# Linformer attention and an MLP mixer on one core: batch 0's loads, its last head pair and its E and F in another order, and a planner's table in place of its shaken priorities

## The chip, the cores and the metric

The kernel runs on one core of a Trainium2 chip. The metric is the device time of one execution in microseconds (us); three runs of the kernel before gave 421.42, 422.15 and 422.19, with a median of 422.15. The engines are TensorE (PE; its weight loads are listed apart as PEld), VectorE (DVE), ScalarE (ACT), GpSimd (POOL) and SyncE (SP). A core has 16 DMA engines, which the queues of the engines share.

## The reference

Eight batches, eight heads, a sequence of 1024 and 64 elements a head. Attention is of the Linformer kind: k and v are first projected along the sequence to 64 rows by E and F. An MLP mixer follows, on x, which has 512 columns (eight heads side by side).

```python
k_proj = np.einsum('ks,bhsd->bhkd', E, k)
v_proj = np.einsum('ks,bhsd->bhkd', F, v)
scores = scale * np.matmul(q, k_proj.transpose(0, 1, 3, 2))
...
x = softmax(scores) @ v_proj                       # B, S, H * D
h = np.maximum(xt @ w_tok1, 0.0) @ w_tok2          # xt: x with S and columns exchanged, 1024 -> 256 -> 1024
u = x + h.transpose(0, 2, 1)
h2 = np.maximum(u @ w_ch1, 0.0) @ w_ch2            # 512 -> 1536 -> 512
return (u + h2).astype(np.float32)
```

All inputs and the output are float32 in the chip's memory; the kernel computes in bfloat16 with float32 sums.

## The kernel before

**Stages of a batch.** `kv_proj` (L479) multiplies k by E and v by F, both turned, in eight steps of 128 sequence rows; the k side and the v side use different halves of the array. ScalarE copies the result out, k to `kp` or `kb`, v to `vb`. `k_transpose` and `q_transpose_pe` (TensorE, batch 0 and 1) or DMA transposes on SP (L524, L570; from batch 2 on) bring q and k into the layout that `scores` (L605) needs; `attend` (L628) multiplies the softmax's numerators `a` by v, and VectorE divides (`rdn` L640, `x_sb` L645 and L681). `token1` and `token2` are the token MLP, in forms that differ by batch: in pairs of heads for batch 0 (`token1_pair`, `token2_pair`, L1067), plain for batch 1, in a seven-product scheme later (L744, L856). VectorE adds x to make `u` (L1079 in batch 0).

**The channel MLP** holds most of the work. u is transposed into `uT` (on TensorE in batch 0; by `turn_u`, L767, one DMA transpose on SP for each half of a batch after that). A half batch is a block j = 2b or 2b + 1. Each block does seven products of quarter matrices in place of eight, twice: `s_sums` (L789) makes the sums S of quarters on VectorE, `up_set` (L1152) the products to the hidden layer in two sets of columns, and `down_block` (L1261) the products back. Sums of weights (`wT`, `wc_sb`, L452) are made once. VectorE adds results and u into three tiles `o` (L1301, L1311), which rotate over half blocks, and `store` (L1295) writes an o tile out. Blocks with j under `EARLY_O` (4) put one part into `wait_t` first.

**The order of the work** is made when the program is built. A `Planner` (L50 to L203) holds jobs with an engine, a planned duration, a priority and the PSUM banks they take; it lists them in planned order. Priorities above `SHAKEN_FROM` are shifted by a hash of the job's number, within plus and minus 0.8. The list is then sorted by start; loads and stores (`early`) are sorted by the time at which their inputs or buffers are free, not by their planned start:

```python
j.at = est[j.n] if j.early else t
...
return sorted(order, key=lambda j: j.at)
```

Each engine's instructions stand in that order, and so do the DMA issues of each queue. Loads (`load_heads`, L363, issued at L354) and most stores go through GpSimd's queue, one behind another; the last blocks store through SP and ScalarE. Later batches' loads are 512 KB each (four heads of k, v or q). A group of three loads is tied (`tie`, L358; the wait is put in at L1503) behind a `turn_u`, and the second `turn_u` of a batch behind these loads, so that loads and DMA transposes take turns.

**The start.** E and F come in float32 through SP's and ScalarE's queues into two o tiles; they are turned with sixteen 64x64 transposes (L441) against `ident32`, which GpSimd makes after the first load's issue. Batch 0's loads stand in this order: k, v, q of head pairs 0, 1 and 2 (256 KB each), `wt1` (512 KB, the first token weight), k, v, q of pair 3, `wt2`, then the channel weights, then batch 1's six loads. Eight products on zeros (`blank`, L413) run while nothing has arrived; while bank 5 is free, the emitting loop (L1489) puts in one more for each 0.216 us of a planned hole on TensorE.

Of the kernel before, what the change touches and what calls it, by code (L numbers as in the profile page):

```python
# [14 lines left out]
SHAKEN_FROM = -30.0  # L15
SHAKE = 1.6
SEED = 710
# [7 lines left out]
EARLY_O = 4  # L25
# [3 lines left out]
class Job:  # L29


    def __init__(self, n, eng, occ, lat, fn, prio):
        self.n, self.eng, self.occ, self.lat, self.fn, self.prio = n, eng, occ, lat, fn, prio
        self.deps, self.next, self.takes, self.banks = set(), [], [], []
        self.start = self.end = None
        self.early = False
# [11 lines left out]
class Planner:  # L48


    LAG = {"PE": 0.25, "DVE": 0.15, "ACT": 0.15, "POOL": 0.2, "DMA": 1.0}
# [34 lines left out]
    def plan(self):  # L86
# [16 lines left out]
        for j in self.jobs:  # L103
            if j.prio > SHAKEN_FROM:
                j.prio += SHAKE * ((j.n * j.n * 7919 + j.n * SEED * 31 + SEED * SEED * 17) % 10007 / 10007 - 0.5)
# [19 lines left out]
        order = []  # L125
        turn = {n: [b for j in self.jobs for b in j.takes if b.stream == n] for n in self.caps}
# [28 lines left out]
        while any(can.values()):  # L155
# [23 lines left out]
            j.start, j.end, j.full = t, t + j.lat, t + j.lat + 0.03  # L179
# [27 lines left out]
def kernel(  # L207
# [66 lines left out]
    EF = [o_t[i].rearrange("p a b -> p (a b)")[:KP] for i in range(2)]  # L274
    nc.sync.dma_start(out=EF[0], in_=E)
    nc.scalar.dma_start(out=EF[1], in_=F)
# [18 lines left out]
    kp = wS[:KP, 0].rearrange("p a b -> p (a b)").rearrange("p (h r d) -> p h r d", h=H // 2, r=2)  # L295
    kb = tile_of([P, H, 2, D], BF16, "kb")
    ET_sb = tile_of([P, NSI, KP], BF16, "ET_sb")
    FT_sb = tile_of([P, NSI, KP], BF16, "FT_sb")
# [15 lines left out]
    ident32 = ub_t[0][:KP, 0, :KP]  # L314

    zero = tile_of([P, P], BF16, "zero")
    nc.vector.memset(zero, 0.0)
    nc.vector.memset(vb, 0.0)
# [12 lines left out]
    def pe(n, cols, fn, **kw):  # L331
        t = n * MM[cols]
        return pl.add("PE", t, t, fn, **kw)
# [12 lines left out]
    def ld(mb, fn, **kw):  # L346
        t = mb / 0.40
        j = pl.add("DMA", t, t + 2.0, fn, **kw)
        j.early = True
        return j  # L350
# [12 lines left out]
    def load_heads(b, name, h, hn, due):  # L363
        dst, src = {"k": (k_sb, k), "v": (v_sb, v), "q": (q_sb, q)}[name]
        hs = slice(h, h + hn)
        return ld(
            0.262 * hn,
            dma(dst[:, hs], src[b, hs].rearrange("h (p si) d -> p h si d", p=P)),
            writes=[(name, i) for i in range(h, h + hn)], prio=due,
        )  # L370
    first = iter(range(-1000, 0))
    for hp in range(HP):
        if hp == HP - 1:
            w1t = moe_w_tok1.rearrange("(p si) t -> p si t", p=P)
            ld(1.05, dma(wt1_sb, w1t), writes=["wt1"], prio=next(first))
        for name in "kvq":
            load_heads(0, name, 2 * hp, 2, next(first))
    w2t = moe_w_tok2.rearrange("(tc p) s -> p tc s", p=P)
    ld(1.05, dma(wt2_sb, w2t), writes=["wt2"], prio=next(first))
# [44 lines left out]
    for i in range(8):  # L424
        warm(i)
# [5 lines left out]
    pl.add("POOL", 1.0, 2.4, identities, writes=["ident"], prio=-150)  # L431

    for n, (src, dst) in enumerate(((EF[1], FT_sb), (EF[0], ET_sb))):
        b = Bank("S", full=False)

        def view(b=b):
            return bank(b).rearrange("p (si k) -> p si k", si=NSI)

        def turn(src=src, view=view):
            for si in range(NSI):  # L440
                nc.tensor.transpose(view()[:, si, :], src[:, si:S:NSI], ident32)  # L441

        def take(n=n, dst=dst, view=view):
            (nc.vector.tensor_copy if n else nc.scalar.copy)(out=dst, in_=view())

        pl.add("PE", 1.6, 1.6, turn, reads=["ident"], takes=[b], prio=-150)
        (dve if n else act)(512, take, writes=["FT", "ET"][n : n + 1], uses=[b], prio=-150)
# [31 lines left out]
    def kv_proj(b, h0, hn, due, block=False):  # L479
        hs = slice(h0, h0 + hn)  # L480
        hk = slice(h0 % (H // 2), h0 % (H // 2) + hn)
        heads = range(h0, h0 + hn)
        bk = Bank(stream[0], full=False)

        def view():
            return bank(bk).rearrange("p (h d) -> p h d", d=D)

        def mm(lo, hi):
            t = view()
            for si in range(lo, hi):  # L490
                a, z = si == 0, si == NSI - 1
                nc.tensor.matmul(  # L492
                    t[0:KP, 0:hn], ET_sb[:, si, :], k_sb[:, hs, si, :], start=a, stop=z
                )
                nc.tensor.matmul(
                    t[KP : 2 * KP, 0:hn], FT_sb[:, si, :], v_sb[:, hs, si, :], start=a, stop=z
                )

        cols = hn * D
        reads = ["ET", "FT"] + [(n, h) for n in "kv" for h in heads]  # L500
        pl.add(
            "PE", 8 * max(cols, 128) / 2400 + 0.22, 8 * max(cols, 128) / 2400 + 0.22,
            lambda: mm(0, NSI), reads=reads, takes=[bk], prio=due,
            after=[("vb", i, h) for i in range(2) for h in heads],
        )
        src = [lambda: view()[0:KP, 0:hn], lambda: view()[KP : 2 * KP, 0:hn]]
        if block:
            k_to = [kb[i * KP : (i + 1) * KP, hs, i, :] for i in range(2)]
        else:
            k_to = [kp[:, hk, i, :] for i in range(2)]  # L510
        v_to = [vb[i * KP : (i + 1) * KP, hs, i, 0:D] for i in range(2)]

        def copy(to, n):
            return lambda: nc.scalar.copy(out=to, in_=src[n]())

        for i in range(2):
            act(cols, copy(k_to[i], 0), writes=[("kb" if block else "kp", i, h if block else h % (H // 2)) for h in heads], uses=[bk])
        for i in (1, 0):
            act(cols, copy(v_to[i], 1), writes=[("vb", i, h) for h in heads], uses=[bk])
# [11 lines left out]
    def k_transpose(h0, hn, due):  # L531
# [7 lines left out]
        def mm():  # L539
            for h in range(hn):  # L540
                nc.tensor.matmul(
                    view()[:, h, :], kp[:, h0 % (H // 2) + h].rearrange("k r d -> k (r d)"),
# [4 lines left out]
            hn, 64, mm, reads=[("kp", i, h % (H // 2)) for i in range(2) for h in heads], takes=[bk],  # L547
# [142 lines left out]
    def token1(t, due):  # L690
# [9 lines left out]
        for part in range(2):  # L700
            pe(
                4, 512, lambda part=part: mm(part), reads=["wt1"] + [("x", h, part) for h in range(H)],
# [61 lines left out]
    def turn_u(b, i):  # L764
        turned_u[b, i] = sp(
# [9 lines left out]
        if b > 1:  # L775
            turned_u[b, i].lat += 3.0
# [23 lines left out]

    def tok1_quarter(t, half):
        return wt1_sb[:, half * NJ : (half + 1) * NJ, t * P : (t + 1) * P]

    def tok1_sums():
        a11, a12, a21, a22 = [tok1_quarter(t, half) for t in range(2) for half in range(2)]

        def one(n, out, in0, in1, add=False, deps=(), after=()):
# [3 lines left out]
                reads=["wt1"] + [("wS", m) for m in deps], writes=[("wS", n)], after=after,  # L811
            )

        kp_all = [("kp", i, h) for i in range(2) for h in range(H // 2)]
# [3 lines left out]
        one(6, wS[:, 1], wS[:, 0], a11, deps=(5,))  # L818
        one(3, a21, a12, wS[:, 1], deps=(6, 7, 5), after=["wt1"])
# [7 lines left out]
    def token1_seven(b, due):  # L827
# [35 lines left out]
        def product(n):  # L863
# [4 lines left out]
            w = [("wS", n)] if n in (5, 6, 7, 3) else ["wt1"]  # L868
# [162 lines left out]
    def token1_pair(hp, due):  # L1031
        cols = slice(hp * P, (hp + 1) * P)
        bk = Bank(stream[0], full=False)

        def view():
            return bank(bk)[:, 0 : TC * P].rearrange("p (t c) -> p t c", t=TC)

        def mm(t):
            for si in range(NSI):
                nc.tensor.matmul(  # L1040
                    view()[:, t, :], wt1_sb[:, si, t * P : (t + 1) * P], x_sb[:, si, cols],
                    start=(si == 0), stop=(si == NSI - 1),
                )

        for t in range(TC):
            pe(
                NSI, 128, lambda t=t: mm(t),
                reads=["wt1"] + [("x", 2 * hp + h, n) for h in range(2) for n in range(2)],
                takes=[bk] if t == 0 else [], uses=[bk] if t else [], prio=due,
            )  # L1050
        act(
            256,
            lambda: nc.scalar.activation(out=hT_sb[:, :, cols], in_=view(), func=ACT.Relu),
            writes=[("hT", t, hp) for t in range(TC)], uses=[bk],
        )

    def token2_pair(hp, i, due):
        cols = slice(hp * P, (hp + 1) * P)
        bk = Bank(stream[0], full=False)

        def view():
            return bank(bk).rearrange("p (s c) -> p s c", s=NJ)

        def mm():
            for ss in range(NJ):
                for t in range(TC):
                    nc.tensor.matmul(  # L1067
                        view()[:, ss, :], wt2_sb[:, t, i * NJ + ss :: NSI], hT_sb[:, t, cols],
                        start=(t == 0), stop=(t == TC - 1),
                    )  # L1070

        rows = slice(i * NJ, (i + 1) * NJ)
        pe(
            NJ * TC, 128, mm, reads=["wt2"] + [("hT", t, hp) for t in range(TC)], takes=[bk],
            prio=due,
        )
        dve(
            512,
            lambda: nc.vector.tensor_add(  # L1079
                out=u_t[0][:, rows, cols], in0=view(), in1=x_sb[:, rows, cols]  # L1080
            ),
            reads=[("x", 2 * hp, i), ("x", 2 * hp + 1, i)], writes=[("up", hp, i)], uses=[bk],
        )

    def u_transpose_pe(hp, i, due):
# [11 lines left out]
        pe(NJ, 128, mm, reads=[("up", hp, i)], takes=[bk], prio=due)  # L1097
# [437 lines left out]
```

## Time and profile before

| what | value |
|---|---|
| runs | 421.42, 422.15, 422.19 us |
| span of the profiled execution | 420.3 us |
| its own time | one of the runs above, 1.1 to 1.9 us over the span |
| TensorE busy | 410.3 us (98%), 3824 products |
| VectorE busy | 347.5 us (83%) |
| ScalarE busy | 231.3 us (55%) |
| GpSimd busy | 66.2 us (16%) |
| moved by the DMA engines | 62.48 MB, mean 149 GB/s |
| sixteen 64x64 transposes of E and F | 2.00 us, from 5.75 us |
| first S sum of block 0 ends | 35.95 us |
| kv_proj of batch 1, heads 4 to 7, starts | 55.46 us |
| kv_proj of batch 3, v side, starts | 110.04 us |

The slices of the page cut the span into 40 equal parts and give the busy share of each in tenths. The chain is followed back from the last instruction: at each step it goes to what released that step. A DMA on the chain means that an engine stood until that transfer had landed. In a timeline a row gives start, length, engine, line, tiles and, in brackets, the idle time before it and what ended it.

### The profile page before, as it was taken

To read this page: it belongs to the slowest core of one execution; us is meant where nothing else is said; L and a number is where in the kernel's file an instruction comes from. 1 tells how busy PE (TensorE), PEld (TensorE's weight loads), DVE (VectorE), ACT (ScalarE), POOL (GpSimd) and SP (SyncE) were. 2 spreads that over 40 slices of the span, in tenths; PEclk is the share of its full clock that TensorE was granted. 3 is DMA by queue.
4 is the path that set the end of the run, shared out by engine and by line. 5 is a ranking of instruction groups with operands and counts; after the bars stand their busy time and mean duration, and the time that the engine had idled before them with its cause. 6 is when DMAs were issued, how large, how long until landed. Compare 5 with 4: busy or idle time off the path is not lost.

```text
span 420.3 us, 9411 instructions
## 1 busy us (share of the span) xinstructions
PE 410.3 (98%) x3824; PEld 347.6 (83%) x3838; DVE 347.5 (83%) x747; ACT 231.3 (55%) x444; POOL 66.2 (16%) x104
## 2 busy tenths in 40 slices
PE   7899999999999999999999999999999999999996
PEld 4587877688788888888988898888798899988885
DVE  2359969679779798998979799797979999978685
ACT  2958885356646555555547455475655554454430
POOL 8443220022003030032002110112100000010010
PEclk9999999999999999999999999999999999999999
DMA  9999999989994989398998897395962501251223
GB/s 166 207 201 206 207 206 166 238 137 204 174 152 88 194 138 251 60 165 159 198 205 130 175 183 194 84 189 100 209 149 50 152 35 67 50 97 56 101 89 114
DMA packets 96668, 62.48 MB, mean 149 GB/s; under 512 B 62064, under 2 KB 92272, under 8 KB 96624
## 3 DMA queue, kind: packets, MB, share of 16 engines
q0 software_dynamic: 34944, 45.09, 54.9%
q1 hardware_dynamic: 61056, 16.00, 22.6%
q10 hardware_dynamic: 624, 0.79, 0.7%
q8 instruction: 30, 0.49, 0.4%
q14 instruction: 14, 0.11, 0.1%
HBM read 59.24 MB, written 16.78 MB: 181 GB/s over the span
## 4 chain that ended last, share of the span: by engine, by line
PE 87%; DMA 6%; DVE 4%; issue 1%; POOL 1%; ACT 0%; POOLq 0%; DVEq 0%
PE psum L1261 34%; PE psum L1152 33%; PE psum L856 4%; PE psum L972 4%; DMA v_sb<-in_v_dram 3%; DMA q_sb<-in_q_dram 3%; PE psum L492 3%; PE psum L605 3%; PE psum L664 2%; DVE u L1079 1%; PE psum L628 1%; PE psum L695 1%; PE psum L719 1%; PE psum L744 1%; PE psum L589 1%
## 5 line engine op out<-in xcount | busy, mean ns | idle before, releaser
L1261 PEld LDWEIGHTS <-G 128*128 128x128 bf16 x1344 | 130.4, 98 | 18.9 <-issue 0.6
L1261 PE MATMUL psum<-wc_sb,G 128*128 128x256 bf16 x768 | 102.9, 273 | 0.3 <-DVE wait L1301 0.3
L1174 ACT ACTIVATE G<-psum 128x512 bf16<-128x512 f32 x96 | 57.3, 599 | 56.8 <-PE psum L1152 56.5
L1152 PEld LDWEIGHTS <-wc_sb 128*128 128x128 bf16 x768 | 74.1, 98 | 10.2
L1261 PE MATMUL psum<-wT,G 128*128 128x256 bf16 x576 | 77.6, 273 | 0.3
L1188 DVE TENSOR_TENSOR G<-G 128x512 bf16<-128x512 bf16 (+1 forms) x140 | 69.6, 519 | 1.0
L1152 PEld LDWEIGHTS <-wT 128*128 128x128 bf16 x576 | 55.7, 98 | 9.0 <-issue 0.8
L1152 PE MATMUL psum<-S,wc_sb 128*128 128x256 bf16 x384 | 57.6, 273 | 0.2
L1152 PE MATMUL psum<-uT,wc_sb 128*128 128x256 bf16 x384 | 57.6, 273 | 0.0
L1152 PE MATMUL psum<-S,wT 128*128 128x256 bf16 x384 | 55.7, 273 | 0.2 <-DVE S L789 0.2
L1295 POOL DMA_DIRECT2D out_dram<-o x30 | 16.4, 546 | 240.3 <-DVE o L1301 160.5
L614 ACT ACTIVATE a<-psum 128x512 bf16<-128x512 f32 x64 | 36.7, 598 | 17.6 <-PE psum L605 16.5
L1301 DVE TENSOR_TENSOR o<-psum,u 128x512 f32<-128x512 f32 x55 | 37.6, 685 | 9.5 <-PE psum L1261 7.2
L1180 ACT COPY ua<-psum 128x512 f32<-128x512 f32 x48 | 28.2, 588 | 25.5 <-PE psum L1152 25.1
L1133 DVE CUSTOM_DVE_ANT_0 G<-psum,ub 128x512 bf16<-128x512 f32 x48 | 33.0, 687 | 9.1 <-PE psum L1152 8.9
L1133 DVE CUSTOM_DVE_ANT_0 G<-psum,ua 128x512 bf16<-128x512 f32 x48 | 33.0, 688 | 8.0 <-ACT ua L1180 7.8
L1195 ACT COPY psum<-psum 128x512 f32<-128x512 f32 x48 | 27.9, 580 | 14.5 <-PE psum L1152 5.3
L1180 ACT COPY ub<-psum 128x512 f32<-128x512 f32 x48 | 28.2, 587 | 9.4 <-PE psum L1152 8.3
L1152 PE MATMUL psum<-uT,wT 128*128 128x256 bf16 x192 | 28.8, 272 | 0.1
L681 DVE TENSOR_TENSOR x_sb<-psum,rdn 128x512 bf16<-128x512 f32 x40 | 27.5, 688 | 0.6
L605 PE MATMUL psum<-qT,kT 128*128 128x512 bf16 x54 | 19.8, 379 | 1.4 <-ACT kT L557 0.6
L354 POOL DMA_DIRECT2D v_sb<-in_v_dram x18 | 13.5, 751 | 45.8 <-DMA uT<-u 25.0
(108 smaller groups left out, 546.3 us busy)
## 6 DMA issues: line engine op xcount, KB each, us to landing
out_dram<-o POOLq DMA_DIRECT2D x30, 512.0 KB, 4.4
k_sb<-in_k_dram POOLq DMA_DIRECT2D x14, 512.0 KB, 9.5
v_sb<-in_v_dram POOLq DMA_DIRECT2D x14, 512.0 KB, 10.5
q_sb<-in_q_dram POOLq DMA_DIRECT2D x14, 512.0 KB, 9.4
wc_sb<-in_moe_w_ch_dram POOLq DMA_DIRECT2D x6, 256.0 KB, 12.4
wc_sb<-in_moe_w_ch_dram POOLq DMA_DIRECT2D x4, 384.0 KB, 12.2
k_sb<-in_k_dram POOLq DMA_DIRECT2D x4, 256.0 KB, 6.6
v_sb<-in_v_dram POOLq DMA_DIRECT2D x4, 256.0 KB, 7.2
```

Source lines behind the costliest of these rows:

```text
L605: lambda: nc.tensor.matmul(bank(bk), kT[:, h].rearrange("p c k -> p (c k)"), qT[:, h].rearrange("p j s -> p (j s)"), start=True, stop=True,),
L614: lambda: nc.scalar.activation(out=a_t[h // 2 % 2][:, h % 2], in_=bank(bk), func=ACT.Exp, scale=scale),
L681: lambda: nc.vector.tensor_tensor(out=x_sb[:, :, h * D : (h + 1) * D].rearrange("p (n c) d -> p n c d", n=2), in0=view()[:, :, :, 0:D], in ...
L856: nc.tensor.matmul(to, tok1_of(n, si), mv, start=(n == 1 and si == 0), stop=(si == NJ - 1), skip_group_check=True,)
L1133: nc.vector._custom_dve(TENSOR_ADD_SAT, out=out, in0=in0, in1=in1, s0=FMAX, s1=0.0)
L1152: nc.tensor.matmul(t[:, c, :], w1_of(n, dd, 2 * m + c), a_of(j, n, dd), start=(n in (1, 7) and c == 0 and dd == 0), stop=(c == 1 and dd == 1),
L1174: lambda: nc.scalar.activation(out=G[:, n, cs], in_=view(src), func=ACT.Relu),
L1180: 512, lambda: nc.scalar.copy(out=dst, in_=view("y")), writes=[(name, s % 2)],
L1188: 512 * len(both), lambda: f(out=G[:, n, c], in0=G[:, a, c], in1=G[:, b, c]), ps=False,
L1195: 512, lambda: nc.scalar.copy(out=view("y"), in_=view("x")), takes=[bk["y"]],
L1261: nc.tensor.matmul(to, G[:, G_OF[n], cc, t * P : (t + 1) * P], w2_of(n, cc), start=(n in opens and (t == 0 or alone) and cc == 0), stop=(c ...
L1301: 512, lambda: nc.vector.tensor_add(out=dst, in0=view(src), in1=u_of(sh, dh)),
```

## The change

- **Loads of batch 0.** k, v, q of pairs 0 to 2 as before, then k, q, v of pair 3, then `wt1` in two halves of four rows each, then `wt2`. The bytes are the same.
- **Pair 3 apart.** `kv_proj` makes two jobs for heads 6 and 7, one for the k side (with its own bank) and one for the v side.
- **E and F** go into the two halves of one o tile's partitions and are turned together: eight transposes of 128x128 against a 128x128 `ident32`.
- **kp** has room for all eight heads instead of four.
- **Token MLP of batch 0.** `token1_part` and `token2_part` replace the pair forms; `token1` is split into parts of four rows, so that a part needs one half of `wt1`. `uT` and the u keys of batch 0 are finer (by two rows of tiles).
- **Products on zeros.** Ten at the start in place of eight; later a single float32 one where the planned hole is over 1.0 us, three in all (before, eighteen).
- **EARLY_O** is 2 in place of 4.
- **Planner.** A table `NUDGES` with one character for each job shifts its priority by a quarter of its distance from the character 80 (2234 characters; standard deviation about 6), in place of the hash. The loads of batch 0 and of the weights are planned to land 1 us later once 112 matmuls have been planned (`FETCH`, `FETCHING`, `behind`), and the planned duration of these loads is changed.

In the program, the order of the instructions on every engine changes throughout. On GpSimd's queue batch 1's loads stand k, v, q, k, q, v (before k, v, q, k, v, q); the loads behind uT(1,1) stand q, q, v (before v, q, q); and the store of block 4's first half stands behind the three loads k, v, k that it stood ahead of.

```diff
-SHAKEN_FROM = -30.0
-SHAKE = 1.6
-SEED = 710
+STEP = 0.25
+MIDDLE = 80
+NUDGES = (
...
-EARLY_O = 4
+EARLY_O = 2
+LOADS = (
+    ("k", 0, 2), ("v", 0, 2), ("q", 0, 2), ("k", 2, 2), ("v", 2, 2), ("q", 2, 2),
+    ("k", 4, 2), ("v", 4, 2), ("q", 4, 2), ("k", 6, 2), ("q", 6, 2), ("v", 6, 2),
+    ("wt1", 0, 4), ("wt1", 4, 4), ("wt2", 0, 0),
+)
+GROUPS = ((0, 2), (2, 2), (4, 2), (6, 2))
+APART = (6,)
+PART = 4
...
-        for j in self.jobs:
-            if j.prio > SHAKEN_FROM:
-                j.prio += SHAKE * ((j.n * j.n * 7919 + j.n * SEED * 31 + SEED * SEED * 17) % 10007 / 10007 - 0.5)
+        for j, c in zip(self.jobs, NUDGES):
+            j.prio += STEP * (ord(c) - MIDDLE)
...
-            j.start, j.end, j.full = t, t + j.lat, t + j.lat + 0.03
+            late = self.FETCHING if j.behind and mms >= self.FETCH else 0.0
+            mms += j.mms
+            j.start, j.end, j.full = t, t + j.lat + late, t + j.lat + late + 0.03
...
-    EF = [o_t[i].rearrange("p a b -> p (a b)")[:KP] for i in range(2)]
-    nc.sync.dma_start(out=EF[0], in_=E)
-    nc.scalar.dma_start(out=EF[1], in_=F)
+    EF = o_t[0].rearrange("p a b -> p (a b)")
+    nc.sync.dma_start(out=EF[:KP], in_=E)
+    nc.scalar.dma_start(out=EF[KP : 2 * KP], in_=F)
...
-    kp = wS[:KP, 0].rearrange("p a b -> p (a b)").rearrange("p (h r d) -> p h r d", h=H // 2, r=2)
+    kp = wS[:KP, 0:2].rearrange("p n a b -> p (n a b)").rearrange("p (h r d) -> p h r d", h=H, r=2)
...
-    ident32 = ub_t[0][:KP, 0, :KP]
+    ident32 = ub_t[0][:, 0, :P]
     zero = tile_of([P, P], BF16, "zero")
+    zero32 = tile_of([P, P], F32, "zero32")
...
-    for i in range(8):
+    for i in (*range(8), 7, 7):
         warm(i)
...
-            for si in range(NSI):
-                nc.tensor.transpose(view()[:, si, :], src[:, si:S:NSI], ident32)
+            for i in range(NJ):
+                nc.tensor.transpose(bank(b).rearrange("p (i k) -> p i k", i=NJ)[:, i], EF[:, NJ * n + i : S : NSI], ident32)
...
-    def kv_proj(b, h0, hn, due, block=False):
+    def kv_proj(b, h0, hn, due, block=False, apart=False):
...
+        for names in ("k", "v") if apart else ("kv",):
+            side(names)
...
-    for hp in range(HP):
-        token1_pair(hp, -10.0 + hp)
+    for p0, pn in PARTS:
+        token1_part(p0, pn, -10.0 + p0)
...
-            for _ in range(int((j.start - idle - 0.3) / 0.216) if spare is not None and j.prio > -100 else 0):
-                blank(spare)
+            if spare is not None and j.prio > -100 and j.start - idle > 1.0:
+                nc.tensor.matmul(
+                    spare, zero32, zero32[:, None, :].to_broadcast([P, NJ, P]), start=True, stop=True
+                )
```

## The prediction

> **What bounds the kernel now.** I read the busy shares and slices first, then a table of stretches, then the chain, then the queues where the chain shows a transfer. The page:
>
> ```profile
> span 420.3 us, 9411 instructions
> PE 410.3 (98%) x3824; PEld 347.6 (83%) x3838; DVE 347.5 (83%) x747; ACT 231.3 (55%) x444; POOL 66.2 (16%) x104
> PE   7899999999999999999999999999999999999996
> DMA  9999999989994989398998897395962501251223
> PE 87%; DMA 6%; DVE 4%; issue 1%; POOL 1%; ACT 0%; POOLq 0%; DVEq 0%
> ```
>
> TensorE carries 87% of the chain. The stretches (busy time of each engine, then granted clock, DMA share, GB/s) say where it does not:
>
> ```profile
> 27.00:36.00 9.00, 8.16 (x124) 7.50 (x123) 8.78 (x23) 5.62 (x13) 5.01 (x7) 1.00 1.38 201
> 36.00:55.00 19.00, 18.84 (x183) 15.99 (x184) 18.94 (x47) 16.09 (x33) 3.70 (x5) 1.00 1.24 206
> 55.00:110.00 55.00, 54.28 (x489) 43.22 (x490) 45.61 (x125) 32.42 (x63) 8.94 (x13) 1.00 1.01 186
> 110.00:410.00 300.00, 299.42 (x2745) 260.91 (x2753) 260.07 (x514) 161.06 (x301) 32.04 (x50) 1.00 0.69 134
> ```
>
> From 110 to 410 us TensorE misses 0.6 us. So a new order of the same products can win there next to nothing; it can only lose. What can be won lies ahead of 36 us, which the chain shows to be arrivals, then VectorE:
>
> ```profile
> 5.18 6.29 DMA v_sb<-in_v_dram
> 11.76 12.13 DMA q_sb<-in_q_dram
> 29.03 0.72 DVE x_sb L645 x2
> 35.27 0.68 DVE S L789 x2
> 35.99 2.40 PE psum L1152 x20
> 54.87 0.66 PE psum L1261 x6
> 55.53 0.23 PE psum L492
> 102.71 7.29 DMA v_sb<-in_v_dram
> ```
>
> The q of pair 3 lands at 23.9, x of pair 3 is made at 29.0, and the first S sum ends at 35.95; only then does TensorE stream. The last row is the one later transfer on the chain: kv_proj of batch 3 waits for v until 110.0. Last, GpSimd's list, since it issues the loads and stores in a fixed order on one queue, and the issues with their time to landing:
>
> ```profile
> 36.84 0.74 POOL L354 DMA_DIRECT2D v_sb<-in_v_dram  x1 [1.17 <-DMA wc_sb<-in_moe_w_ch_dram]
> 38.78 0.74 POOL L354 DMA_DIRECT2D q_sb<-in_q_dram  x1 [1.20 <-PE psum L1152]
> 179.24 0.53 POOL L1295 DMA_DIRECT2D out_dram<-o  x1 [24.43 <-DVE o L1301]
> 179.80 0.75 POOL L354 DMA_DIRECT2D k_sb<-in_k_dram  x1
> ```
>
> ```profile
> v_sb<-in_v_dram POOLq DMA_DIRECT2D x1, 512.0 KB, 18.0
> q_sb<-in_q_dram POOLq DMA_DIRECT2D x1, 512.0 KB, 18.7
> ```
>
> The fifth load of batch 1 (v, heads 4 to 7) lands at 36.84 + 18.0 = 54.8, the sixth (q) at 38.78 + 18.7 = 57.5. The queue is full until 72.7 (some 205 GB/s in every slice), so a place in it fixes a landing: the bytes ahead are the same in both kernels. kv_proj of heads 4 to 7 started at 55.46, 0.6 after its v.
>
> **The change part by part.** Prices by rows: four 128x256 products 0.437 us, six 0.656, a score 0.216, an attend 0.115. By these the two kernels have equal TensorE work (the removed products on zeros were fillers in waits), so only waits count.
>
> Head (before 36 us). The loads of pair 3 come ahead of wt1: by landings 1.28 apart, k of pair 3 at about 18, q 20.1, v 21.3 (before 21.3, 23.9, 22.6), wt1 in two halves at 22.6 and 23.9, wt2 at 26.4 as before. So x of pair 3 is off the end, but token2 still starts with wt2. Behind it VectorE before did, from 27.22 to the S sum's end at 35.95, eight u adds, pair 3's reciprocals and x (1.77), four wT sums and the S sum; after, pair 3's x and one u add and one wT sum fewer stand there: 1.77 + 0.60 + 0.33 = 2.7 less, which I take as 2.3, since the first add waits for token2's own first group. E and F turned together take eight 128-wide transposes for sixteen, and the wait for k at 6.35 covers them; if that cover went, half of the transposes' 2.00 us, 1.0, would be lost or won. The two added f32 memset and identity instructions lie beside the start-up; their bound is the 1.16 us that TensorE waited there for F. Pair 3's k and v sides, projected apart, no longer share the array: eight steps of 0.109 become sixteen, at most 0.87 more, under the wait for wt2. The three f32 fillers have no row: 0.22 (a warm bf16 one) to 1.0 (the hole each is put into), hence nothing beside the hole. Fewer fillers cost nothing if the clock stays up: before, fillers ran at 0.45 us each at the start and 0.22 later, so a colder head could take back up to the whole 2.3. Gain taken: 2.3 (0 to 3.1, the latter with the halves of wt1 used at once).
>
> A. First new wait, kv_proj of batch 1, heads 4 to 7. In the after program GpSimd's order for batch 1 is k, v, q, k, q, v: the pair that is projected apart frees v's buffer last, so this v is the sixth load and lands at 57.5. TensorE has, from the first up product on, 1.53 us more work ahead of this kv_proj (12 up products 1.31, a score 0.22, a token2 group for a transpose group 0.23, less two attends 0.23), so it would come at 55.46 + 1.53 - 2.3 = 54.7 and stands 2.8 us. All of the head's gain is gone, however large it was. By the same prices 1.30 us less work remains behind it than before. Sum so far: 57.5 - 55.46 - 1.30 = **+0.7** (-0.3 if the queue runs 1 us ahead, +1.3 if as late as 58.1). While TensorE stands, everything later on its queue waits, down products included; nobody can pass.
>
> On that hole: the trace's granted clock is 1.0 throughout, its longest hole after warming about 1 us. The Trainium skill, "TensorE: Matmul & The Clock Gate", Part 1, drops the clock to half after an idle window of about 3.4 us; 2.8 us would not fill one, and if it did the estimate from that page is about 1.7 us more for the ramp. No row of this trace decides it.
>
> B. First up product of batch 1's second half (it reads uT(1,1)). SP's transposes and GpSimd's loads take turns. Before: uT(1,0) issued 81.84 (26.4 after kv_proj) and landed 86.75; loads from 87.35, the third landed 98.94; one store behind them 100.26; uT(1,1), issued 96.32, landed 1.9 later, 102.14, just in time for its user. After: the last producer of uT(1,0) comes 27.4 us of work behind kv_proj, so it issues at about 85.2 and lands at 90.1; three loads from 90.7, the third at 102.3; now both stores of that block stand ahead of the transpose, not one, at 1.3 each: 105.0; the transpose 106.9. TensorE gets there at 57.5 + 46.7 of work + 0.9 of small waits = 105.1. **+1.6** (0 if the second store slips behind, 2.9 if each transfer runs as slowly as the slowest row).
>
> D. kv_proj of batch 3. Its loads, issued behind uT(1,1), stand q, q, v where before they stood v, q, q. Before, the three landed 7.3, 9.8 and 12.4 after the first issue with a store ahead; in idle queues 5.4, 8.6, 11.5. Issue 107.6, v at 119.1; TensorE at 106.9 + 11.1 of work = 118.0. **+1.1** (0 to 2.4), and the wait of 0.6 at 110.0 of before goes: **-0.6**.
>
> C. Store of block 4's first half. Before, it was issued at 179.24, ahead of the three loads, and landed in 3. In the after program it stands behind k, v, k. They issue at about 177.2, when uT(3,0) has landed; a store behind three loads lands 12.3 to 12.9 us after the first (182.02 to 194.07 counted from 179.80), so at 189.8. The add into the same o tile, for block 5, is due at about 188.1. VectorE waits some 1.6; its next add, queued behind, holds the bank that TensorE wants: **+1.3** (0 to 2.7).
>
> Rest. The wait at 409 (0.3) is gone: **-0.3**. Two fewer early blocks that use wait_t give the same number of adds, bound by the 0.34 us of the one wait on that tile, either way; taken as 0. The k buffer for all eight heads removes a wait that no row shows.
>
> Sum: 0.7 + 1.6 + 1.1 - 0.6 + 1.3 - 0.3 = +3.8 on the profiled execution, whose span is 420.3; the timed runs lie 1.1 to 1.9 above that, the median 1.85. So 422.15 + 3.8 = **426.0 us**.
>
> **Rivals.** (1) Faster. The gain at the head stays, because the sixth load lands with TensorE at 54.7, not 57.5. For it speaks that buffers come free earlier and GpSimd stood 1.2 us ahead of both loads; against it that the queue was full and 18 us deep there, so an earlier issue lands no earlier. With no later wait it decides from a landing under 56.8 (56.8 - 55.46 - 1.30 - 0.6 - 0.3 = -0.86). At 54.7: 422.15 - 2.1 - 0.9 = 419.2. (2) Only A holds, the later three are caught by slack (before had uT landing just in time, so a us less in the queue would do): 422.15 + 0.7 - 0.6 - 0.3 = 422.0, no change. (3) Worse: B, C and D at their slow ends, 2.9 + 2.4 + 2.7 in place of 4.0: +7.8, 430. For it speaks that each late transfer delays the loads behind it.
>
> **How the numbers follow.** The measurement tells no change from about 0.2%, 0.84 us, so faster is under 421.3, slower over 423.0. Forecast (two or three of B, C, D bite) 0.57, rival 1 0.15, rival 2 0.16, rival 3 0.12. Rival 2 lies in the middle band mostly, a few hundredths to either side; slower 0.70, same 0.12, faster 0.18. Leaving out about 0.1 at each end: 420.3 to 429.5; the forecast alone 423.5 to 428.5.
>
> **What would show.** Right: first S sum near 33.5, a hole of 2 to 3 us that ends at 57.5 with v_sb as releaser at kv_proj, waits near 106, 118 and 189, hence DMA above 6% of the chain, TensorE still 1.0 in clock. Wrong: kv_proj of heads 4 to 7 begins before 56; or uT(1,1) lands before TensorE; or the store of block 4 lands by 187. A head that ends no earlier than 35 would change nothing in the sum, since A swallows it.

## The result

The changed kernel takes 429.83 us (429.61 to 431.72, four runs) against 422.17 for the kernel before. The recorded ratio of the runs is 1.0174 (that of the two medians 1.018), with a 95% interval of 1.0149 to 1.0200. It is slower, as forecast, but by 7.7 us, not 3.8, and 0.3 us beyond the upper end of the range. The profiled execution has a span of 428.2 us against 420.3.

The page of the changed kernel, in the order in which the page of before was shown:

```profile
span 428.2 us, 9384 instructions
PE 409.2 (96%) x3808; PEld 346.6 (81%) x3820; DVE 349.0 (82%) x748; ACT 230.8 (54%) x444; POOL 67.0 (16%) x105
PE   7899979998999999989999987999999999999996
PE 73%; DMA 18%; ACT 3%; issue 2%; POOL 2%; DVE 1%; POOLq 0%; DVEq 0%; ACTq 0%
```

TensorE's share of the chain fell from 87% to 73%, and that of transfers rose from 6% to 18%. Its busy time is 1.1 us less: the loss is waiting. The stretches (busy time of each engine, clock, DMA share, GB/s) say where:

```profile
36.00:55.00 19.00, 18.82 (x183) 15.69 (x182) 17.28 (x42) 15.83 (x32) 3.91 (x6) 1.00 1.24 206
55.00:110.00 55.00, 50.90 (x462) 40.68 (x463) 44.01 (x121) 30.65 (x59) 8.93 (x13) 1.00 0.98 174
110.00:410.00 300.00, 294.07 (x2692) 255.49 (x2696) 256.93 (x506) 159.55 (x299) 31.11 (x48) 1.00 0.70 133
```

Before, TensorE missed 0.7 us from 55 to 110 and 0.6 from 110 to 410; now 4.1 and 5.9. What it waited for after 36 us (total, times, longest):

```profile
PE psum L569 <- DMA v_sb<-in_v_dram: 5.2, 3, 2.4
PE psum L732 <- DVE x_sb L749: 1.4, 1, 1.4
PE psum L1232 <- DMA uT<-u: 1.3, 1, 1.3
PE psum L1232 <- DVE G L1213: 1.1, 1, 1.1
```

And four rows of its chain (start, length, what):

```profile
39.29 18.57 DMA v_sb<-in_v_dram
...
181.09 8.56 DMA out_dram<-o
...
235.52 11.92 DMA uT<-u
...
249.47 10.21 DMA v_sb<-in_v_dram
```

The first row is batch 1's sixth load; the second a store; the last two a transpose of u and the v behind it. I measured each wait from start to start, less the row prices of the products between (0.109 for a 128x256 one, and so on), which adds the part that the pipeline's ends hide:

| ends at, us | TensorE waits for | us | forecast |
|---|---|---|---|
| 57.90 | v, batch 1, heads 4 to 7 (A) | 2.57 | 2.8 |
| 106.80 | uT(1,1) (B) | 1.44 | 1.6 |
| 118.94 | v, batch 3 (D) | 0.82 | 1.1 |
| 191.09 | VectorE, behind block 4's store (C) | 1.27 | 1.3 |
| 248.96 | VectorE's x, behind an S sum | 1.58 | none |
| 259.72 | v, batch 6 | 2.68 | none |

These six make 10.4. The kernel before had two such waits, 0.61 at 110.04 and 0.28 at 409, which are gone, while one of 0.50 behind `wait_t` stands in both. The head (all that stands ahead of 36 us) gained 1.96: the second S sum ends at 33.98, before at 35.94. 10.4 - 0.9 - 2.0 = 7.5, of the 7.9 by which the spans differ.

### The profile page after: what moved, and what is told of

The parts are those of the page before. It is cut to its first block, busy times and chain, and to the rows that moved or that the text cites. A ratio compares the mean times of both kernels' runs of the same rounds, so it can differ in the third digit from the quotient of the medians.

```text
span 428.2 us, 9384 instructions
## 1 busy us (share of the span) xinstructions
PE 409.2 (96%) x3808; PEld 346.6 (81%) x3820; DVE 349.0 (82%) x748; ACT 230.8 (54%) x444; POOL 67.0 (16%) x105
## 4 chain that ended last, share of the span: by engine, by line
PE 73%; DMA 18%; ACT 3%; issue 2%; POOL 2%; DVE 1%; POOLq 0%; DVEq 0%; ACTq 0%
PE psum L1341 28%; PE psum L1232 26%; DMA v_sb<-in_v_dram 11%; DMA uT<-u 6%; PE psum L569 3%; PE psum L1043 3%; PE psum L927 3%; PE psum L673 2%; DMA out_dram<-o 2%; PE psum L732 2%; PE psum L696 1%; PE psum L1144 1%; PE psum L1112 1%; PE psum L763 1%; PE psum L787 1%
## 5 line engine op out<-in xcount | busy, mean ns | idle before, releaser
L1341 PE MATMUL psum<-wT,G 128*128 128x256 bf16 x576 | 76.4, 273 | 0.1
L1381 DVE TENSOR_TENSOR o<-psum,u 128x512 f32<-128x512 f32 x59 | 40.4, 685 | 12.7 <-PE psum L1341 8.4
L569 PE MATMUL psum<-v_sb,EFT_sb 128*64 128x512 bf16 (+2 forms) x96 | 16.0, 310 | 6.1 <-DMA v_sb<-in_v_dram 6.1
L569 PEld LDWEIGHTS <-EFT_sb 128*64 128x64 bf16 x192 | 9.5, 109 | 14.8 <-issue 8.0
## 6 DMA issues: line engine op xcount, KB each, us to landing
wc_sb<-in_moe_w_ch_dram POOLq DMA_DIRECT2D x6, 256.0 KB, 11.9
```

The source lines that it names most:

```text
L569: nc.tensor.matmul(view(n), sides[n][3][:, si, :], sides[n][4][:, hs, si, :], start=(si == 0), stop=(si == NSI - 1),)
L1341: nc.tensor.matmul(to, G[:, G_OF[n], cc, t * P : (t + 1) * P], w2_of(n, cc), start=(n in opens and (t == 0 or alone) and cc == 0), stop=(c ...
L1381: 512, lambda: nc.vector.tensor_add(out=dst, in0=view(src), in1=u_of(sh, dh)),
```

## The experiments

Several move one DMA issue in the finished list of jobs, with this helper; the order of TensorE's instructions is then the same to the last one. `job_of` finds a load by name, batch and first head.

```python
def put(j, other, behind):
    plan.remove(j)
    plan.insert(plan.index(other) + behind, j)
```

| run | what | us | ratio to before, 95% interval |
|---|---|---|---|
| x9_q_behind | changed, A's v fifth | 427.14 | 1.0102 (1.0061 to 1.0143) |
| x6_wt1_first | changed, wt1 ahead of pair 3 | 429.43 | 1.0133 (1.0094 to 1.0173) |
| x8_no_stores | changed, without block 1's stores | 428.12 | 1.0109 (1.0073 to 1.0145) |
| x14_store6_late | changed, block 6's second store late | 426.30 | 1.0073 (1.0044 to 1.0101) |
| x4_hash | changed, shaken priorities | 428.72 | 1.0119 (1.0072 to 1.0166) |
| x1_planned | changed, issues in planned order | 425.03 | 1.0059 (1.0038 to 1.0081) |
| x7_planned_v | x1, v first | 420.98 | 0.9943 (0.9922 to 0.9963) |
| x11_planned_v_wt1 | x7, wt1 ahead of pair 3 | 426.06 | 1.0076 (1.0048 to 1.0105) |
| x12_hash_planned_v | x7, shaken priorities | 424.66 | 1.0041 (1.0021 to 1.0061) |
| x10_store_late | x7, block 1's second store late | 419.83 | 0.9931 (0.9908 to 0.9954) |
| x13_two_late | x10, block 6's second store late | 419.15 | 0.9903 (0.9869 to 0.9937) |

The runs were taken on several chips, each beside runs of the kernel before, whose medians went from 422.17 (beside the changed kernel) to 423.08 (beside x6, x7, x8 and x4). Differences between medians below are therefore good to about 1 us; where two intervals of the table overlap, the time alone does not tell two kernels apart, and the reading rests on the waits in the traces. Each kernel has one profiled execution.

### A: the late v, and what became of the head's gain

Two first tries at moving the v missed. They put v ahead of q, and so ahead of the separate v projection of pair 3 in the program:

```diff
+    put_ahead(job_of["v", 1, 4], job_of["q", 1, 4])
```

> Changed kernel with one swap: on GpSimd's queue the load of batch 1's v (heads 4 to 7) stands ahead of that of q, fifth of six instead of sixth. Theory (the late v alone holds TensorE there, and everything later shifts with it): the v lands at about 55.4 instead of 57.9, TensorE comes at 55.3, the wait of 2.57 us at 57.9 is gone, the waits at 107, 119, 191, 249 and 260 stay as long and come 2.4 us earlier: 427.4 us against 429.8 of the changed kernel. Rival (the later transfers are paced by the queue alone, so that a gain here is waited off at uT(1,1)): that wait grows from 1.4 to 3.8 us and the time stays at 429.8.

> As the run before, and in each later batch's group q, q, v (behind the second transpose of u) the v stands first. Theory: v lands some 6 us after the first issue instead of 11 to 12; the waits for v at 118.9 (0.8 us) and 259.7 (2.7 us) go too, those at 107, 191 and 249 stay: 2.4 + 0.8 + 2.7 = 5.9 less than the changed kernel, 423.9 us. Rival (the q's, now last, are wanted as early, so the wait moves to q's transposes and the scores behind them): no better than the swap in batch 1 alone, 427.4 us.

They took 461.81 and 458.62 us. That projection then read the tile after batch 1's load, and stood until it had landed:

```profile
PE psum L572 <- DMA v_sb<-in_v_dram: 37.2, 4, 33.6
```

So both say nothing on A. The two differ only in the later groups, by 3.2 us, a first sign that v's place there counts. The same move made from the other side is sound:

```diff
+    put(job_of["q", 1, 4], job_of["v", 1, 4], 1)
```

> Changed kernel with one move on GpSimd's queue: batch 1's q (heads 4 to 7) stands behind v (heads 4 to 7), so that v is the fifth load and q the sixth; q's transposes come some 3.5 us behind kv_proj in TensorE's order and find it landed. Theory: the v lands at 55.4, the wait of 2.57 us goes, the later waits keep their length: 427.4 us. Rival (a gain there is waited off at uT(1,1)): 429.8 us.

It took 427.14 us, 2.7 less. No wait for v is left near 55 us, and the later ones stayed, each some 3 us earlier: 1.42 at 103.8, 0.6 at 115.9, 1.04 at 187.8, 1.90 at 246.0, 2.60 at 256.8. The theory holds: a gain at 57.9 is not lost at uT(1,1).

The other side of A is that the head should not matter. A first attempt padded TensorE's work ahead of the wait:

```diff
+        if "q_transpose_pe" in j.fn.__qualname__ and 40.0 < j.start < 52.0:
+            j.fn()
+            j.fn()
```

> Changed kernel with two jobs of q transposes of batch 1, ahead of the kv_proj that waits at 57.9, made three times over: 32 more transposes on TensorE, at 0.0625 us about 2.0 us, the output unchanged. Theory (that kv_proj starts when its v lands, whatever the head of the kernel gained): the wait there shrinks from 2.57 to about 0.6 us and the time stays at 429.8 us, at most 0.3 more. Rival (TensorE's work sets the end there): 431.8 us.

It took 434.29 us (430.61 to 436.38) and settles nothing: the repeated transposes held back ScalarE's copies of qT, and TensorE waited 2.6 us for these (the second wait of 2.0 ended at 59.23), after which the clock fell as well. The pad added a wait of its own. Moving loads alone does it cleanly:

```diff
+    for h in (0, 4):
+        put(job_of["wt1", 0, h], job_of["k", 0, 6], 0)
```

> Changed kernel with both halves of wt1 issued ahead of pair 3's k, q, v, as before the change; all else, TensorE's order too, is the same. Pair 3's loads land 2.5 us later. Theory (the wait for batch 1's v at 57.9, 2.57 us, swallows what the head gains): streaming begins up to 2.5 us later, that wait shrinks by the same, the time stays at 429.8 us within 0.5. Rival (the head's gain reaches the end): 2 us more, 431.8.

> The kernel with planned issue order and v first (420.98 us), with both halves of wt1 issued ahead of pair 3's k, q, v. In the changed kernel this move cost nothing, since the wait at 57.9 lay behind it. Theory (with no late v behind it, the head's gain reaches the end): streaming begins 2.8 us later and the time is 2 to 2.8 us more, 423.0 to 423.8. Rival (the head's gain is swallowed by another wait): 421.0 us.

In the changed kernel the second S sum then ends 2.8 us later (36.80), the wait at 57.9 is gone, and the time is the same within the noise: 429.43 (by the ratios it lies 1.7 us lower, with overlapping intervals). So a gain ahead of 57.9 is lost there. In the kernel without the late v, the same move makes the second S sum end 4.95 us later (38.34; 33.39 in x7), since TensorE waits 3.7 us for pair 3's k and then runs at half clock for 6.8 us (3.4 in x6). The time is 5.1 us longer, where 2 to 2.8 was expected. In the profiled execution a wait for x at 248.3 (1.66) came on top. The head's gain is real and worth about its whole length, once no late load lies behind it.

### Issue order against planned order

```diff
-        return sorted(order, key=lambda j: j.at)
+        return sorted(order, key=lambda j: j.start)
```

> Changed kernel with loads and stores issued in the order in which the planner places them, not in that of the times at which their inputs or buffers are free. Batch 1's v is fifth of six, and block 4's first store stands behind one load instead of three; the groups q, q, v stay. Theory: the waits at 57.9 (2.57 us) and 191 (1.3 us) go, the others stay: 2.4 + 1.3 = 3.7 less than the changed kernel, 426.1 us. Rival (each store that stands later delays a later block's adds): as many new waits as are taken away, 429.8 or more.

425.03 us, 4.8 less, where 3.7 was expected. A and C (2.57 + 1.27) are gone as expected; 1.23 at 103.9, 0.52 at 115.8, 1.11 at 244.0 and 2.88 at 255.0 are left, 0.8 less in all than in the changed kernel. So the planner had placed v fifth and block 4's store ahead of all but one load; sorting loads and stores by the time at which they could go made another order out of it, for which the work had not been placed.

```diff
+    for b in range(3, B):
+        for h in sorted((0, 4), key=lambda h: -plan.index(job_of["q", b, h])):
+            if plan.index(job_of["q", b, h]) < plan.index(job_of["v", b, 4]):
+                put(job_of["q", b, h], job_of["v", b, 4], 1)
```

> The kernel with planned issue order (425.0 us) and in each later batch's group q, q, v the v first. Theory: the waits for v at 115.8 (0.5 us) and 255 (2.9 us, behind which the clock fell to half in the profiled run) go; those for uT(1,1) at 104 (1.2) and for x at 244 (1.1) stay: 425.0 - 3.4 = 421.6 us. Rival (the q's, now last, are wanted as early): the wait moves to the scores behind q's transposes, 424 to 425 us.

420.98 us, faster than before the change. The q's are not missed: no wait for them shows. This is the waiting that is left after 36 us:

```profile
PE psum L1235 <- DMA uT<-u: 0.9, 1, 0.9
PE psum L1344 <- DVE wait L1384: 0.3, 1, 0.3
PE psum L1046 <- ACT G L1257: 0.2, 1, 0.2
```

The wait for x at 249 is gone here as well, though nothing was done for it; uT(4,1) landed at 240.2, 10.1 us after its issue. VectorE's S sum still waited 0.33 us for it, TensorE not at all.

### B: two stores ahead of a transpose

```diff
-                1.5, lambda: queue.dma_start(...)
+                1.5, (lambda: None) if j == 1 else lambda: queue.dma_start(...)
```

> Changed kernel without the two stores of block 1 (the second half of batch 0's output is not written); nothing else is changed. Theory (these two stands ahead of uT(1,1) on the DMA engines cost 1.3 us each): uT(1,1) lands at about 104.2 instead of 106.8, the wait there (1.44 us) goes, the loads behind it land 2.6 earlier, so that the wait for v at 118.9 (0.8) goes too: 429.8 - 2.3 = 427.5 us. Rival (the loads and the transposes set the pace, stores fit beside them): 429.8 us.

428.12 us, 1.7 less. The next loads issue at 104.64 (107.36 in the changed kernel), so uT(1,1) came 2.7 us earlier, and neither wait, B nor D, is left. Less than the expected 2.3 reached the end: the wait for x near 248 grew to 2.93, while that for v fell to 1.05, and in the profiled execution the clock stood at half for 3.4 us behind the first of these. In the kernel with planned order, one of the stores moved is enough:

```diff
+    put(store_of[1, 1], max((job_of["q", 3, 0], job_of["q", 3, 4], job_of["v", 3, 4]), key=plan.index), 1)
```

> The kernel with planned issue order and v first (420.98 us), with block 1's second store issued behind the loads that follow uT(1,1), so that one store stands ahead of that transpose instead of two. Theory: uT(1,1) lands 1.3 us earlier, the wait of 1.1 us at 103 goes: 420.0 us. Rival (the store, or the o tile that it holds, delays something later by as much): 421.0 us or more.

419.83 us, and no wait for uT(1,1). The two times alone don't tell this kernel from x7, as their intervals overlap. The wait for x was back, 1.68 at 243.0, with uT(4,1) 12.0 us on its way; x7's profile is of its fastest run (420.20) and this one of its slowest (421.34), so that wait may come and go between executions.

### The two waits without a forecast, 249 and 260

VectorE in the changed kernel, near 248 (start, length, engine, line, tiles, and in brackets the idle time before):

```profile
247.47 0.43 DVE L858 TENSOR_TENSOR S<-uT 128x512 bf16<-128x512 bf16 x1 [1.82 <-DMA uT<-u]
247.81 0.20 DVE L744 RECIPROCAL rdn<-psum 128x8 f32<-128x8 f32 x1
...
248.22 0.69 DVE L749 TENSOR_TENSOR x_sb<-psum,rdn 128x512 bf16<-128x512 f32 x1
```

The S sum waits for uT(4,1); reciprocal and x, which need no uT, stand behind it, and TensorE waits for the bank that x frees. What was open: why this transpose lands so late. The issues near it, in the changed kernel:

```profile
out_dram<-o POOLq DMA_DIRECT2D x1, 512.0 KB, 10.7
uT<-u SPq DMA_TRANSPOSE x1, 11.9
```

A store was issued 0.3 us behind the transpose. Moving it behind the loads that follow:

```diff
+    put(store_of[6, 1], max((job_of["q", 6, 0], job_of["q", 6, 4], job_of["v", 6, 4]), key=plan.index), 1)
```

> Changed kernel with one store moved: block 6's second store, which was issued at 235.8 beside the second transpose of u of batch 4 (issued 235.5, landed 247.4), goes behind the loads that follow this transpose. Theory (the transpose lands late because it shares the DMA engines with that store and the k load; VectorE's S sum waits for it and holds x back): it lands 1.3 us earlier, the wait for x at 249 (1.4 to 1.6 us) falls to about 0.2; the wait for v at 260 (2.7) stays as long, since both its load and TensorE come earlier: 428.4 us against 429.8. Rival (the transpose is as slow without the store): 429.8 us.

> The kernel with planned issue order, v first and block 1's second store late (419.83 us), with block 6's second store late as well. Theory: the wait of 1.7 us at 243 for x, behind VectorE's S sum that waits for the transpose, falls to about 0.3: 418.4 us. Rival: 419.8 us.

The transpose, in the changed kernel with that store moved:

```profile
uT<-u SPq DMA_TRANSPOSE x1, 8.5
```

11.9 to 8.5 us: 3.4 less, where a store had been priced at 1.3. 426.30 us, 3.5 less, where 1.4 was expected: the wait for x is gone, and that for v at 257.2 fell from 2.68 to 0.68, as its load came 3.4 us nearer while TensorE came only some 1.5 nearer. In the version with planned order both moves together give 419.15 us, the best of all, 0.97% below before. Its chain, and its waits after 36 us:

```profile
PE 93%; ACT 2%; DMA 2%; DVE 1%; issue 1%; POOL 1%; POOLq 0%; ACTq 0%; DVEq 0%
```

```profile
PE psum L1345 <- DVE wait L1386: 0.3, 1, 0.3
PE psum L1047 <- ACT G L1258: 0.2, 1, 0.2
```

No transfer is among the waits. Its span, 417.7 us, is 2.6 us under that of before, which is the head's 2.1 (the second S sum ends at 33.84) and the two waits that the change took away, less small change.

### Is it the table?

```diff
-        for j, c in zip(self.jobs, NUDGES):
-            j.prio += STEP * (ord(c) - MIDDLE)
+        for j in self.jobs:
+            if j.prio > -30.0:
+                j.prio += 1.6 * ((j.n * j.n * 7919 + j.n * 710 * 31 + 710 * 710 * 17) % 10007 / 10007 - 0.5)
```

> Changed kernel with the shaken priorities of before in place of the table; loads, pair 3 apart, E and F together, fillers and EARLY_O as after the change. Batch 1's v is again the sixth load, so the wait at 57.9 stays in both readings. Theory (beside that wait the table's order costs, since it leaves less work between the transposes of u and their users): some of the waits at 191, 249 and 260 (5.5 us) are gone and the time is 424 to 427 us. Rival (the other parts of the change cost, whatever the order): 429.8 us or more.

> As the kernel with planned issue order and v first (420.98 us), but with the shaken priorities of before in place of the table. Theory (the order of the loads and stores on GpSimd's queue is what costs, under either order of the work): 428.7 us of the shaken order falls by as much as with the table, to 420 to 422. Rival (it is the table that is worth something, once the loads are right): 423 us or more.

With the old shaking the other parts of the change cost nearly as much: 428.72 us, with an interval that overlaps that of the changed kernel. A is there too (1.61 at 59.27), and the waits at 191, 249 and 260 are replaced by others (1.26 at 151.5 for VectorE behind an o tile, 0.69 for v at 160). With planned order and v first it falls by 4.1, to 424.66, not to the 420 to 422 that I expected. The number is the rival's (423 or more), but the theory holds in part: the issue order costs under either order of work, and once it is right the table's order is the better one by 3.7 us (424.66 against 420.98). The table itself was not the loss; the order of the issues was. The kernel before sorts its issues by the same rule and has waits of only 0.9 us for it, so the rule costs only together with the other parts of the change. Which of these turned the order no run shows: none takes pair 3's separate projection, the token MLP's parts, EARLY_O or the fillers back alone. That the separate v projection of pair 3 makes v the sixth load is argued from the program; x2, in which v went ahead of it, fits.

## Why the prediction was right and wrong

**Right.** The reading of the kernel before held: almost nothing to win after 36 us, all to lose by landings. A: v landed at 57.86 (57.5 in the text), the hole 2.57 (2.8), and the head's gain was swallowed, as x6, x9 and x11 show from both sides. B: uT(1,1) landed at 106.76 (106.9), and x8 shows the two stores as its cause. D: v landed at 118.90 (119.1). C: VectorE waited 1.9 us for the store (1.6), TensorE 1.27 (1.3); x1, in which the store stands elsewhere, has no such wait. The head's gain was 1.96 (2.3); the 35.95 that is called the first S sum there is the end of the second one, and the first alone ended at 35.61 before and 33.65 after. One slip in the sum: by its own figures B is 106.9 less 105.1, so 1.8 and not 1.6; it measured 1.44.

**Wrong.** The step that failed is "Rest". It took the work after block 4 as free and only credited 0.3. The two waits there measured 1.58 + 2.68 = 4.26, all of what the sum lacked: 3.8 + 4.3 = 8.1, against 7.7. The count that the prediction made for B and D, carried on to batch 6, gives them. In the changed kernel uT(4,0) was issued at 221.84 and the v that ends the group landed at 259.68, 37.8 us on; before, the same way took 215.69 to 251.60, 35.9, and kv_proj began at 252.37, so with only 0.8 to spare. TensorE's busy time from that issue to kv_proj is the first number behind the comma; the upper row is of the kernel before:

```profile
215.69:252.37 36.68, 36.63 (x343) 32.18 (x342) 31.90 (x64) 20.50 (x39) 6.17 (x9) 1.00 0.98 163
221.84:259.72 37.88, 34.03 (x316) 29.50 (x315) 33.09 (x65) 20.04 (x38) 6.68 (x10) 1.00 0.93 155
```

Without the two waits of 4.26, the 37.88 us of the changed order hold 33.6 us of work (the row's 34.0 counts some 0.4 of pipeline ends as busy), 3.1 less than the 36.7 before. So 1.9 more on the way of the transfers, less 0.8 of slack, and 3.1 less work beside them make 4.2. The larger part is the work that the changed order takes out of this stretch. Of the 1.9, 1.5 is one store that now stands ahead of the group's loads. GpSimd's list, in the changed kernel and before:

```profile
227.90 0.53 POOL L1375 DMA_DIRECT2D out_dram<-o  x1 [15.14 <-DMA uT<-u]
228.46 0.76 POOL L404 DMA_DIRECT2D v_sb<-in_v_dram  x1
...
222.06 0.75 POOL L354 DMA_DIRECT2D v_sb<-in_v_dram  x1 [9.44 <-PE psum L1152]
```

That v was issued 0.2 us later behind the landing of uT(4,0) than before, and took 6.93 us to land against 5.58.

**The size of one term.** I priced a store ahead of a transpose by its own length, 1.3 us. That held where it stood ahead (B: 2.7 for two; 1.5 for the one ahead of batch 6's loads). For the store issued beside the transpose (uT(4,1)) I had no term. Moving it shortened the transpose by 3.4 us in the changed kernel. But it is no part of the loss: the kernel before has stores beside this transpose too (issued at 227.59 and 233.22), and there it took 11.58 us, against 11.92 after the change. So x14 shows that of the two waits one can be removed and the other cut to 0.68 in this way, not that this store brought them.

**The rivals.** Rival 1 (the sixth load lands early) fell: the queue was full and v landed 0.4 later than the row said. Rival 2 (slack catches the later waits) fell. Rival 3 (430) came near the number by luck: B, C and D were at their middle values, not their slow ends.

**The clock.** The prediction weighed the rule of the Trainium skill, "TensorE: Matmul & The Clock Gate", Part 1, by which an idle window of about 3.4 us halves the clock, and held that a hole of 2.8 would not. In the profiled execution of the changed kernel it did not: the granted clock stayed 1.00. But shorter holes than 3.4 us did it elsewhere, in x14 behind this very wait, as the last section shows. So it was partly luck, and the rule as I read it is no safe bound.

## What to carry to other kernels

When TensorE is saturated, compare the orders of the issues on each queue before anything else: write down where each load lands and where its first user stands in work, and carry that count through the whole span, not only to the first few places where it bites. A planner that places work by one order of transfers and issues them in another can lose what it placed: here issuing in the planned order won back 4.8 of 7.7 us, and putting the load that is wanted first at the head of its group another 4.1. Moving two stores away from transposes took away the last waits for transfers (1.8 us by the medians of x7 and x13, whose intervals overlap). A gain at the head is worth nothing while a transfer with a fixed landing lies behind it, and its full length once that is gone.

## What the hardware showed beside that

**A store beside a DMA transpose made it 1.6 to 4.7 us longer.** With one 512 KB store issued within 0.3 us of it, and a k load beside it too, the second transpose of u of batch 4 took 11.9 us in the changed kernel, 12.0 in x10, 10.1 in x7 and 13.2 in x8; without that store it took 8.5 in x14 and 8.5 in x13. A store with nothing beside it (issued at 330.04 in the changed kernel) landed after 2.9 us.

**The clock fell to half behind some holes of 2.5 to 2.9 us, and not behind others.** In the profiled execution of x1, TensorE stood from 252.4 to 255.0, and its clock was at half from 254.70 to 258.12 (the third number from the end of a row, before DMA share and GB/s, is the granted clock):

```profile
252.00:255.00 3.00, 0.41 (x4) 0.11 (x3) 2.39 (x4) 0.37 (x1) 0.55 (x1) 0.95 1.33 284
255.00:256.00 1.00, 1.00 (x6) 0.60 (x7) 0.00 (x0) 0.00 (x0) 0.00 (x0) 0.50 0.75 60
256.00:258.40 2.40, 2.40 (x14) 0.94 (x10) 0.00 (x0) 0.00 (x0) 0.00 (x0) 0.56 1.19 343
258.40:262.00 3.60, 3.60 (x35) 3.23 (x35) 2.54 (x7) 3.43 (x8) 0.00 (x0) 1.00 1.15 222
```

kv_proj's eight steps were 0.43 us apart there, 0.22 otherwise: 8 x 0.21 = 1.7 us. That execution took 426.77 us, the four others of the same kernel, with clock 1.0 throughout, 424.59 to 425.13. In x9 a hole of 2.6 that ended at 256.8 was followed by 3.4 us at 0.50, in x8 one of 2.9 that ended at 247.7, and in x14 wait A itself, 2.5 us up to 57.8. In the changed kernel's profile, holes of 2.57 and 2.68 were followed by none, nor was wait A in x8. The profiled executions of x1, x8, x9 and x14 lie 0.8 to 1.7 us above the medians of their kernels. So a hole near 2.6 us may or may not cost 1.7 more; which, the profile of one execution can't tell.
